# Attention with exponentials on two engines: two polynomial steps instead of three, and a looser limit on late fillers

## The chip, the core and the metric

The kernel runs on one core of a Trainium2 chip. A core has five engines that work side by side, each on its own queue of instructions and in order, and that wait for one another through semaphores: TensorE (PE in the profile, with its weight loads as PEld) for matmuls, VectorE (DVE) and ScalarE (ACT) for work on columns of up to 128 partitions, GpSimd (POOL), and SyncE (SP), which here issues DMA transfers. Matmul results land in PSUM, a small memory of eight banks of 512 fp32 columns per partition; all else lies in SBUF.

The metric is the device time in microseconds of one execution. The time before is 905.64 us, the median of 3 runs (905.61 to 906.5).

## The reference

One input x of 2048 tokens by 640 features goes through two halves, and a gate for each token mixes them. Inputs are bf16.

```python
def _A_ref(x, wqkv, wo):
    B, S, D = x.shape
    H = 32; Dh = D // H
    qkv = (lambda x, *d: x.transpose(*d))((x @ wqkv).reshape(B, S, 3, H, Dh), 2, 0, 3, 1, 4)
    q, k, v = qkv[0], qkv[1], qkv[2]
    scores = jnp.einsum("bhqd,bhkd->bhqk", q, k) * Dh ** -0.5
    p = _softmax(scores, axis=-1)
    o = jnp.einsum("bhqk,bhkd->bhqd", p, v)
    return (lambda x, *d: x.transpose(*d))(o, 0, 2, 1, 3).reshape(B, S, D) @ wo
def _B_ref(x, w1, b1, w2):
    h = jnp.einsum("bsd,df->bsf", x, w1) + b1
    sp = jnp.log1p(jnp.exp(-jnp.abs(h))) + jnp.where(h > 0, h, jnp.zeros_like(h))
    act = h * jnp.tanh(sp)
    return jnp.einsum("bsf,fd->bsd", act, w2)
x = A_x
g = _sigmoid((x * gate_w).sum(-1, keepdims=True))
return g * _A_ref(...) + (1 - g) * _B_ref(...)
```

Attention has 32 heads of 20 features each. Its softmax needs 32 x 2048 x 2048 exponentials, far more than anything else in the kernel asks of ScalarE or VectorE. The dense half has 1536 hidden features.

## The kernel before

**Units and steps.** Scores are computed transposed: keys on the 128 partitions, 512 queries in the columns. One such tile of one head is a *unit*: four blocks of queries (c), eight groups of four heads (g), sixteen tiles of keys (kt) and four heads in a group (j) make 2048 units. A *step* holds three units, which lie in three PSUM banks; two sets of three banks take turns. There are 683 steps, the last of two units. For each step, TensorE writes three scores (`emit_s`, line 1059), ScalarE takes the exponential of the step in one instruction (`emit_e`, line 1081), and TensorE multiplies the results by V into one PSUM bank, the four heads of a key tile side by side (`pv`, line 1184). V has a column of ones, so the sum for the softmax's denominator comes with it. When a group ends, VectorE copies the sums out and the group is divided by its denominators (`group_done`).

**Units on VectorE.** In some steps ScalarE takes only two of the three units, and VectorE computes the third exponential. Such a unit goes through these VectorE instructions, each over 512 columns (`emit_x`, from line 1092):
- the eviction (line 1098): score times a scale plus a bias, from PSUM to SBUF. The bias is chosen such that the bits of the fp32 result hold the exponential's exponent and a straight line in place of its mantissa;
- the mask (line 1113): the fraction, the low 14 bits of that word;
- three polynomial steps (line 1115): m = (m + constant) * m;
- the last step (line 1116): m times a small constant plus the evicted word, to an integer whose low 16 bits are the exponential in bf16.

The chains of two units run side by side in two lanes, on the scratch tiles EM and ER. The evicted words lie in five buffers, two of them in XE and three in a region that holds weights at another time: W2R at first, and REG later. The scores two steps later need the bank of the third unit, and so wait for the eviction as well as for ScalarE (`ev_op` in `emit_s`). The product of a finished unit with V is put in by `emit_off` in passes of its own.

**Who fixes the order.** The order of all instructions on all engines is worked out when the program is built. The class `Plan` keeps a clock for each engine, with a planned duration for each kind of instruction (0.60 for a wide VectorE instruction, 0.335 for a fast one, 1.335 for an exponential of three tiles and 0.908 for one of two), and records operations and what they depend on. The waits that are needed follow from that. So the durations in the source do not run on the chip, but they settle which instruction stands where in its queue.

**Fillers.** All other matmuls are tasks that are slipped in between scores and products: the projections for K, Q and V (`kq_task`, `k_task`, `v_pair_task` and their like), which are forced at the step in which they are due, squares for a bound on the scores (`sq_task`), the dense half's two products (`h_task`, `b_task`) and the output product (`p_task`, `part_task`). Their results are evicted by VectorE, and the activation of the dense half is a tanh on ScalarE (line 873) with a dozen VectorE instructions (`mish`). In each step the planner adds up the work of the tasks that can run, divides it by the steps left until each is due, and keeps the largest quotient as `behind`, in microseconds of TensorE work for a step.

**When a unit goes to VectorE.** While the first head group is worked on, `choose` alone decides: a buffer must be free, the work that lies queued for VectorE must be under 7 us, and the unit's chain must end before its group does; otherwise a unit of the next group may be taken. After that three more conditions stand before it: `behind` under `CATCH_UP`, no task more than 8 steps late, and enough VectorE time left for all that is still owed (`room`):

```python
compose(step + 2, choose(step + 2) if fast and step >= CALM and (step < slot_of(0, 1, 0)
        or behind < CATCH_UP and lag < LAG and room()) else None)
```

**Keeping TensorE's clock up.** `fill_up` repeats scores, or multiplies into a free bank, where the planned TensorE work of the last 3.41 us would fall under a share of 0.47.

A second program for scores too large for this method stands behind a flag; it isn't run with these inputs.

Of the kernel before, what the change touches and what calls it, by code (L numbers as in the profile page):

```python
# [64 lines left out]
AHEAD = 14  # L65
BEHIND = 7.0
PATIENCE = 10.0
CATCH_UP = 3.0
BUSY = 0.6
CROWD = 1.4  # L70
MARGIN = 0.5
# [24 lines left out]
ULPS = 128 / math.log(2)  # L96
BIAS = 65536 + 128 * 127
FRACTION = 0x3FFF
STEPS = (125802.5582306, -2329534004.47, 1.968676069154e20)
LAST_STEP = 4.153394027873e-38  # L100


class Op:
# [107 lines left out]
def bass_gated_mix__softmax_full_mha__dense_activation_mish__prompt_kernel(  # L211
# [91 lines left out]
    def ei(home):  # L303

        area, b = home
        return XE[:, b - 3, :] if b >= 3 else AREAS[area][1][:, b * CW:(b + 1) * CW]
# [13 lines left out]
    def scores(s):  # L320
        return PS[:, SLOT * (s % 2):SLOT * (s % 2 + 1), :]
# [7 lines left out]
    def attention(pl, fast):  # L329
# [48 lines left out]
        def slot_of(c, g, kt):  # L378
            return (first_unit[(c, g)] + kt * HG) // SLOT
# [6 lines left out]
        def dve(fn, deps=(), cost=0.1, kind="F"):  # L386

            ready = max([pl.now["dve"], *(d.t1 + HOP for d in deps if d is not None)])
            work(ready + (LATER if fast and now["rate"] < BUSY and now["bank"] else SLACK))
            return pl.add("dve", fn, deps, cost=cost, kind=kind)  # L390
# [638 lines left out]
        def compose(s, extra=None):  # L1029

            if extra:
                order.remove(extra)
                slots[s] = [order.popleft(), order.popleft(), extra]
            else:
                slots[s] = [order.popleft() for _ in range(min(SLOT, len(order)))]

        def emit_s(s):
            deps = [e_op.get(s - 2), ev_op.get(s - 2)]
            deps += [bank_free.get(SLOT * (s % 2) + i) for i in range(SLOT)] if s < 2 else []
            for c, g, kt, j in slots[s]:  # L1040
                if fast:
                    deps += [k_done[(real(g), subs(c, g, kt)[-1][0] // 4)], q_done[(real(g), c)]]
                if fast and (c, g) == (0, 0) and 2 <= kt < 4:
                    deps += k_more
            s_op[s] = score_mms(s, slots[s], deps)
            if any(u[0] < 2 for u in slots[s]):
                low_last[0] = s_op[s]
# [44 lines left out]
        def emit_x(s):  # L1092

            c, g, _, _ = slots[s][2]
            b = off[s]
            x = ei(b)
            y = x.bitcast(FP32)
            ev_op[s] = dve(lambda e: e.tensor_scalar(y, scores(s)[:, 2, :], SCALE * ULPS, BIAS, ALU.mult, ALU.add), [  # L1098
                s_op[s], ei_free[b], *(wkv_read if b[0] else ())], WIDE)
            last = [ev_op[s]]  # L1100
            ei_free[b] = "busy"
            lane = (nx[0] - 1) % LANES
            m = (EM, ER)[lane][:, :]
            f = m.bitcast(I32)
            ends = max((i for i, v in enumerate(islice(order, 80)) if v[:2] == (c, g)), default=0)
            due = pl.now["act"] + ends / TAKEN * EXP

            def piece(cost, fn, deps=lambda: ()):
                def run():
                    last[0] = pl.add("dve", fn, [last[0], *deps()], cost=cost)  # L1110
                soon[lane].append((cost, run, lambda: last[0], due))

            piece(FAST, lambda e: e.tensor_scalar(f, x, FRACTION, None, ALU.bitwise_and), lambda: [lane_last[lane]])
            for i in range(3):
                piece(WIDE, lambda e, v=m if i else f, i=i: e.scalar_tensor_tensor(m, v, STEPS[i], v, ALU.add, ALU.mult))  # L1115
            piece(WIDE, lambda e: e.scalar_tensor_tensor(x, m, LAST_STEP, y, ALU.mult, ALU.add))

            def end():
                lane_last[lane] = unit_done[slots[s][2]] = last[0]
            soon[lane].append((0.0, end, None, due))  # L1120

        def choose(s):

            late = max(0.0, pl.now["dve"] - pl.now["act"])
            urgent, other = (sum(t[0] for todo in some for t in todo) for some in ((norm, *soon), (blend, bg)))
            if (len(order) < SLOT or ei_free[home()] == "busy"
                    or late + urgent + other >= BEHIND):
                return None
            u = order[2]
            ends = max(i for i, v in enumerate(islice(order, 80)) if v[:2] == u[:2])  # L1130
            left = ends / TAKEN * EXP
            before = sum(t[0] for t in blend if t[3] < pl.now["act"] + left)
            if (late + urgent + before + CHAIN) * CROWD + MARGIN >= left:
                n = place[u[:2]] + 1
                js = [v[3] for v in islice(order, 2)]
                later_on = [v for v in islice(order, 3, 80) if n < len(groups) and v[:2] == groups[n] and v[2] < 2 and v[3] not in js]
                if not later_on:
                    return None
                u = later_on[0]
                need = [k_done.get((real(u[1]), 0)), q_done.get((real(u[1]), u[0]))]  # L1140
                if any(op is None or safe(op) > pl.now["pe"] for op in need):
                    return None
            off[s] = off_home[u] = home()
            nx[0] += 1
            off_units.setdefault(u[:2], []).append(u)
            return u
# [264 lines left out]
        def room():  # L1411

            step = now["step"]
            if step < start:
                return True
            owing = sum(t.dve for t in tasks) + sum(t[0] for todo in (norm, *soon, blend, bg) for t in todo)
            owing += 2 * MISH * len(acts) + GROUP * (len(order) // (NKT * HG) + 1) + CHAIN
            return owing + max(0.0, pl.now["dve"] - pl.now["act"]) < LOAD * (NSLOT - LAST - step) * EXP
# [35 lines left out]
        for step in range(NSLOT + 40):  # L1454
# [29 lines left out]
            if step + 2 < NSLOT:  # L1484
                compose(step + 2, choose(step + 2) if fast and step >= CALM and (step < slot_of(0, 1, 0) or behind < CATCH_UP and lag < LAG and room()) else None)
                emit_s(step + 2)
                to_come = pv_ready() * PASS
                if owed + rate > 0.1 and pick(pl.now["pe"] + 0.8):
                    to_come += min(owed + rate, 0.4)
                fill_up(to_come, False)  # L1490

                if fast and step + 2 in off:
                    emit_x(step + 2)
# [182 lines left out]
```

## Time and profile before

| | before |
|---|---|
| median of 3 runs | 905.64 us (905.61 to 906.5) |
| the profiled execution's own time | 901.96 us |
| its span, first to last instruction | 900.1 us |
| granted TensorE clock, mean | 0.995 |
| units on VectorE, of 2048 | 143 |

All views below come from one profiled execution, whose span is 1.86 us shorter than its own time. The page gives the busy time of each engine, its share of the span and the number of its instructions. A row of a group gives the line of the source, engine, operation, output and inputs by name, shapes and count; behind the first bar the busy time in us and the mean ns of one, behind the second the idle time of the engine before it and what ended that. Two instructions of one engine can overlap, so a mean duration may be longer than the distance between two starts; a row of one line of the source gives the first and the last start as well. A row of waits reads: engine, what it wrote, line, what it waited for, then us in total, times, and the longest. Rows of the order of time begin with the start in us from the start of the span and a length.

### The profile page before, as it was taken

What the parts mean: (1) busy time and instruction counts of PE and PEld (TensorE: products, weight loads), DVE (VectorE), ACT (ScalarE), POOL (GpSimd) and SP (SyncE); (2) the same over time, 40 slices, a digit from 0 to 9 for tenths busy, and PEclk for the clock granted to TensorE, in tenths of its full rate; (3) what the DMA queues carried; (4) which work ended last, traced back from release to release, by engine and by line L of the source; (5) the groups of instructions that cost most, each with busy time, mean ns of one, the idle gap of its engine ahead of it and who ended that gap; (6) DMA issues with size and microseconds to landing.
All of it is one profiled execution on the core that took longest, in us unless ns stands there. A gap on an engine that the chain in (4) does not pass through costs nothing.

```text
span 900.1 us, 15301 instructions
## 1 busy us (share of the span) xinstructions
PE 742.2 (82%) x6222; PEld 258.1 (29%) x6265; DVE 840.9 (93%) x1519; ACT 883.2 (98%) x714; POOL 15.3 (2%) x29
## 2 busy tenths in 40 slices
PE   8888778888888888788877878888888878888885
PEld 3222222222322233222222223232332323232232
DVE  5999999989799999999999999999999999979696
ACT  6999999999999999999999999999999999999996
POOL 2000000000000000000000000000000000000000
PEclk9999999999999999999999999999999999999999
DMA  9011200012022111031211120111221201200001
GB/s 215 22 48 55 67 24 13 3 34 68 25 66 77 57 45 42 13 110 32 56 36 43 53 72 19 54 39 32 58 60 42 65 20 54 60 20 24 15 13 35
DMA packets 69871, 42.45 MB, mean 47 GB/s; under 512 B 20472, under 2 KB 65776, under 8 KB 69744
## 3 DMA queue, kind: packets, MB, share of 16 engines
q1 hardware_dynamic: 67424, 40.89, 16.3%
q8 instruction: 52, 0.85, 0.4%
q10 hardware_dynamic: 2256, 0.47, 0.3%
q0 software_dynamic: 112, 0.01, 0.1%
q14 instruction: 27, 0.22, 0.1%
HBM read 33.97 MB, written 5.23 MB: 44 GB/s over the span
## 4 chain that ended last, share of the span: by engine, by line
ACT 95%; PE 2%; DMA 1%; DVE 1%; issue 0%; SPq 0%; ACTq 0%
ACT ETS L1081 92%; ACT REG L873 2%; DMA KT<-KS 1%; ACT W2R L873 1%; PE PS L1059 1%; DMA OTN<-in_A_x_dram 1%; PE PS L1184 0%; PE PS L910 0%; DVE HB L940 0%; PE PS L534 0%; PE PS L645 0%; DVE T L893 0%; DMA SUMS<-RR 0%; PE PS L654 0%; PE PS L934 0%
## 5 line engine op out<-in xcount | busy, mean ns | idle before, releaser
L1081 ACT ACTIVATE ETS<-PS 128x1536 bf16<-128x1536 f32 (+1 forms) x683 | 865.8, 1619 | 2.1 <-PE PS L1059 2.1
L1059 PE MATMUL PS<-QT,KT 32*128 32x512 bf16 (+1 forms) x2231 | 279.0, 378 | 142.3 <-ACT ETS L1081 127.9
L1184 PE MATMUL PS<-ETS,V_all 128*21 128x512 bf16 (+1 forms) x1963 | 211.6, 380 | 0.4 <-ACT ETS L1081 0.4
L1059 PEld LDWEIGHTS PS<-QT,KT 32*128 32x128 bf16 x2231 | 68.8, 91 | 355.4 <-ACT ETS L1081 334.5
L1115 DVE SCALAR_TENSOR_TENSOR EM<-EM 128x512 f32<-128x512 f32 (+1 forms) x216 | 146.9, 680 | 0.4
L1115 DVE SCALAR_TENSOR_TENSOR ER<-ER 128x512 f32<-128x512 f32 (+1 forms) x213 | 145.2, 682 | 0.2
L1184 PEld LDWEIGHTS PS<-ETS,V_all 128*21 128x21 bf16 x1963 | 49.7, 89 | 101.1 <-issue 96.0
L910 PE MATMUL PS<-W2R,HB 128*128 128x320 bf16 x384 | 73.2, 305 | 0.2 <-DVE XS L917 0.2
L841 PE MATMUL PS<-XB,REG 128*128 128x256 bf16 x360 | 53.6, 275 | 0.7 <-DVE HB L851 0.5
L534 PE MATMUL PS<-XB,WOQ 128*128 128x512 bf16 x135 | 41.9, 387 | 2.5 <-issue 1.6
L1098 DVE TENSOR_SCALAR XE<-PS 128x512 f32<-128x512 f32 x56 | 38.3, 684 | 5.2 <-PE PS L1059 5.0
L893 DVE RECIPROCAL T<-T 128x256 f32<-128x256 f32 x24 | 41.8, 1743 | 0.0
L910 PEld LDWEIGHTS PS<-W2R,HB 128*128 128x128 bf16 x384 | 29.7, 98 | 38.1 <-issue 24.3
L841 PEld LDWEIGHTS PS<-XB,REG 128*128 128x128 bf16 x360 | 29.4, 97 | 24.1 <-issue 21.8
L1098 DVE TENSOR_SCALAR REG<-PS 128x512 f32<-128x512 f32 x51 | 34.7, 681 | 1.7 <-PE PS L1059 1.4
L851 DVE TENSOR_TENSOR HB<-PS,B1F 128x512 bf16<-128x512 f32 x48 | 32.8, 683 | 2.4 <-PE PS L841 2.3
L1098 DVE TENSOR_SCALAR W2R<-PS 128x512 f32<-128x512 f32 x36 | 24.6, 684 | 5.1 <-PE PS L1059 4.7
L934 PE MATMUL PS<-WOQ,QT 128*128 128x320 bf16 x128 | 24.2, 302 | 1.1 <-DVE QT L1255 0.9
L934 PE MATMUL PS<-WOQ,OTN 128*128 128x320 bf16 x128 | 24.7, 302 | 0.3 <-DVE HB L851 0.3
L546 DVE CAST QT<-PS 128x512 bf16<-128x512 f32 x31 | 21.3, 686 | 3.1 <-PE PS L534 2.6
L707 PE MATMUL PS<-REG,XB 128*128 128x160 bf16 (+1 forms) x240 | 23.8, 234 | 0.3 <-DVE QT L546 0.2
L873 ACT ACTIVATE REG<-HB 128x1024 f32<-128x1024 bf16 x18 | 23.8, 1321 | 0.0
(124 smaller groups left out, 706.5 us busy)
## 6 DMA issues: line engine op xcount, KB each, us to landing
REG<-in_B_w_dram SPq DMA_DIRECT2D x36, 320.0 KB, 3.2
BCT<-SUMS SPq DMA_DIRECT2D x31, 256.0 KB
W2R<-in_B_w_dram SPq DMA_DIRECT2D x12, 320.0 KB, 3.3
KT<-KS SPq DMA_DIRECT2D x28, 128.0 KB
KS<-OTN SPq DMA_DIRECT2D x16, 128.0 KB, 1.7
W2R<-in_B_w_dram SPq DMA_DIRECT2D x1, 1920.0 KB, 8.3
out_dram<-OUTT SPq DMA_DIRECT2D x24, 80.0 KB, 1.6
REG<-in_A_wqkv_dram SPq DMA_DIRECT2D x2, 700.0 KB, 8.1
```

The costliest lines, as they stand in the source:

```text
L534: return lambda e, bank: e.matmul(PS[:, bank, :], pads[:, b, f, :], xt(c)[:, f, :], start=(f == 0), stop=(f == NFT - 1))
L841: return lambda e, bank: e.matmul(PS[:, bank, i * HW:(i + 1) * HW], w1b(n1)[:, f, i * P:(i + 1) * P], xt(c)[:, f, cols], start=(f == 0), s ...
L851: ev = dve(lambda e: e.tensor_tensor(hb, PS[:, bank, :].rearrange("p (i t) -> p i t", i=2), bias, ALU.add), [last, *b1f, *sq_read.values() ...
L873: ex = pl.add("act", lambda e: e.activation(U, h, AF.Tanh, scale=0.5), [ev, u_free[0]], cost=0.95)
L893: piece(RECIP, lambda e: e.reciprocal(T1[:, :], T1[:, :]))
L910: return lambda e, bank: e.matmul(PS[:, bank, 0:HALF], HB[:, hc % 2, f, t * P:(t + 1) * P], W2[:, f, half * HALF:(half + 1) * HALF], start ...
L934: return lambda e, bank: e.matmul(PS[:, bank, 0:HALF], otn(c, g, fast)[:, t * P:(t + 1) * P], WOG[:, g, half * HALF:(half + 1) * HALF], st ...
L1059: op = pl.add("pe", lambda e, i=i, g=real(g), tile=tile, j=j, cols=cols, c=c, of_q=of_q: e.matmul(scores(s)[:, i, cols], KT[32 * j:32 * j ...
L1081: e_op[s] = pl.add("act", lambda e: e.activation(ETS[:, s % NETS, 0:n, :], scores(s)[:, 0:n, :], AF.Exp, scale=SCALE), [s_op[s], pv_slot.g ...
L1098: ev_op[s] = dve(lambda e: e.tensor_scalar(y, scores(s)[:, 2, :], SCALE * ULPS, BIAS, ALU.mult, ALU.add), [s_op[s], ei_free[b], *(wkv_read ...
L1115: piece(WIDE, lambda e, v=m if i else f, i=i: e.scalar_tensor_tensor(m, v, STEPS[i], v, ALU.add, ALU.mult))
L1184: lasts[n] = pl.add("pe", lambda e, tile=tile, h=real(g) * HG + j, j=j, src=src[:, cols], of_q=of_q, count=count: e.matmul(PS[32 * j:32 * ...
```

## The change

VectorE's exponential loses one of its three polynomial steps; the constants of the two that stay and of the last step are others. The limit on `behind` up to which the planner still gives units to VectorE goes from 3 to 5. The plan that is built from this holds 169 units on VectorE, where it held 143. Planned durations, and the estimate of 3.6 us for a unit's chain in `choose` and `room` (`CHAIN`), are as they were.

```diff
-CATCH_UP = 3.0
+CATCH_UP = 5.0
...
-STEPS = (125802.5582306, -2329534004.47, 1.968676069154e20)
-LAST_STEP = 4.153394027873e-38
+STEPS = (128704.944057677, -2377933447.215862)
+LAST_STEP = 7.799623844033764e-18
...
             piece(FAST, lambda e: e.tensor_scalar(f, x, FRACTION, None, ALU.bitwise_and), lambda: [lane_last[lane]])
-            for i in range(3):
+            for i in range(len(STEPS)):
                 piece(WIDE, lambda e, v=m if i else f, i=i: e.scalar_tensor_tensor(m, v, STEPS[i], v, ALU.add, ALU.mult))
             piece(WIDE, lambda e: e.scalar_tensor_tensor(x, m, LAST_STEP, y, ALU.mult, ALU.add))
```

## The prediction, made before the result was known

> **What bounds the kernel now.** I read the head of the page first, then the chain of the work that ended last.
>
> ```profile
> span 900.1 us, 15301 instructions
> ...
> PE 742.2 (82%) x6222; PEld 258.1 (29%) x6265; DVE 840.9 (93%) x1519; ACT 883.2 (98%) x714; POOL 15.3 (2%) x29
> ...
> ACT 95%; PE 2%; DMA 1%; DVE 1%; issue 0%; SPq 0%; ACTq 0%
> ```
>
> ScalarE (ACT) is busy 98% of the span, and 95% of the chain lies on it. VectorE (DVE) is close behind at 93%, and PE has room. Who waited for whom says the same.
>
> ```profile
> PEld PS L1059 <- ACT ETS L1081: 334.5, 599, 1.5
> ...
> PE PS L1059 <- ACT ETS L1081: 127.9, 280, 1.2
> ...
> ACT ETS L1081 <- PE PS L1059: 2.1, 6, 0.5
> ...
> PE PS L1059 <- DVE XE L1098: 1.0, 2, 0.6
> ```
>
> TensorE stands before the score matmuls for ACT some 600 times. ACT stood idle for scores only six times, 2.1 us in all. So the span is a start, a train of exponentials, and an end. The train by its two forms (and one row of TensorE that is needed further down), in the grouping that keeps shapes apart, then the polynomial steps from the page's costliest groups:
>
> ```profile
> L1081 ACT ACTIVATE ETS<-PS 128x1536 bf16<-128x1536 f32 x539 | 775.5, 1708 | 1.5 <-PE PS L1059 1.5
> ...
> L1081 ACT ACTIVATE ETS<-PS 128x1024 bf16<-128x1024 f32 x144 | 181.5, 1289 | 0.6 <-PE PS L1059 0.6
> ...
> L1184 PE MATMUL PS<-XE,V_all 128*21 128x512 bf16 x54 | 18.3, 400 | 0.0
> ```
>
> ```profile
> L1115 DVE SCALAR_TENSOR_TENSOR EM<-EM 128x512 f32<-128x512 f32 (+1 forms) x216 | 146.9, 680 | 0.4
> L1115 DVE SCALAR_TENSOR_TENSOR ER<-ER 128x512 f32<-128x512 f32 (+1 forms) x213 | 145.2, 682 | 0.2
> ```
>
> 216 + 213 = 429 polynomial steps, three for each of 143 units on DVE. A unit that DVE takes turns a three-tile exponential (1536 columns, a triple) into a two-tile one (1024, a pair). 143 pairs, plus the last step, which has two tiles left (2048 = 682 x 3 + 2), give the 144 of the row.
>
> The mean durations (1708, 1289 ns) overlap from one instruction to the next, so they are no price. I take starts instead, from the rows of line 1081: first the whole run, then a stretch of triples alone, then a mixed stretch without a visible stall.
>
> ```profile
> L1081 ACT ACTIVATE ETS<-PS x683: 1015/1709/2079, 10.4 to 890.3; 128x1536 bf16<-128x1536 f32 x136, 128x1024 bf16<-128x1024 f32 x35
> ```
>
> ```profile
> L1081 ACT ACTIVATE ETS<-PS x19: 1452/1567/1687, 823.2 to 847.1; 128x1536 bf16<-128x1536 f32 x19
> ```
>
> ```profile
> L1081 ACT ACTIVATE ETS<-PS x48: 1092/1692/1816, 37.8 to 95.9; 128x1536 bf16<-128x1536 f32 x37, 128x1024 bf16<-128x1024 f32 x11
> ```
>
> ```profile
> L873 ACT ACTIVATE REG<-HB x18: 1047/1354/1588, 448.0 to 821.3; 128x1024 f32<-128x1024 bf16 x18
> L873 ACT ACTIVATE W2R<-HB x6: 1051/1330/1423, 209.3 to 364.8; 128x1024 f32<-128x1024 bf16 x6
> ```
>
> ```profile
> 448.46 0.94 ACT REG L873
> ```
>
> A triple: 23.9 us over 18 intervals, 1.33 us. A pair without stalls: 58.1 us hold 36 triples and 11 pairs (the last start, a triple, opens no interval), so (58.1 - 47.9)/11 = 0.93 us. A pair on average: 879.9 us from first to last start, less 24 tanh at 0.94 = 22.6, leaves 857.3; less 539 x 1.33 = 716.9 leaves 140.4 for 143 pairs, 0.98 us. Every stall of the train is in that 0.98, wherever it fell.
>
> **The change part by part.**
>
> *The step taken out.* 143 x 1 polynomial step leave DVE. DVE's order of time, in a dense place, gives the price:
>
> ```profile
> 769.92 0.68 DVE L1098 TENSOR_SCALAR REG<-PS 128x512 f32<-128x512 f32 x1
> 770.52 0.68 DVE L903 SCALAR_TENSOR_TENSOR HB<-REG,HB 128x512 bf16<-128x512 f32 x1
> ...
> 771.72 0.42 DVE L1113 TENSOR_SCALAR ER<-XE 128x512 int32<-128x512 int32 x1
> 772.05 0.68 DVE L1115 SCALAR_TENSOR_TENSOR EM<-EM 128x512 f32<-128x512 f32 x1
> 772.66 0.68 DVE L1115 SCALAR_TENSOR_TENSOR ER<-ER 128x512 f32<-128x512 int32 x1
> ```
>
> Starts are 0.60 us apart after a wide instruction and 0.33 after the mask of line 1113. A unit (eviction, mask, three steps, last step) costs 5 x 0.60 + 0.33 = 3.33 us, and 2.73 after. DVE is rid of 143 x 0.60 = 86 us. By itself this moves the end by nothing: ACT's train hides it, and ACT waits for DVE only through TensorE (1.0 us, row above). That the two new constants stand for three changes no shape and no time.
>
> *The 26 units more.* They cost DVE 26 x 2.73 = 71 us, less than the 86 set free, so its load falls by 15 us. Is there room where it is needed? By stage, after the time columns come PE, PEld, DVE, ACT:
>
> ```profile
> 10.00:200.00 190.00, 155.06 (x1333) 49.78 (x1352) 171.98 (x326) 189.10 (x153) 6.52 (x12) 0.99 0.18 48
> 200.00:340.00 140.00, 116.69 (x967) 41.20 (x979) 130.54 (x234) 139.36 (x113) 3.21 (x6) 1.00 0.19 55
> 340.00:700.00 360.00, 297.95 (x2424) 102.89 (x2432) 356.13 (x638) 359.79 (x292) 0.52 (x1) 1.00 0.17 48
> 700.00:892.00 192.00, 162.73 (x1452) 59.50 (x1455) 173.98 (x309) 191.35 (x153) 0.00 (x0) 1.00 0.11 33
> ```
>
> From 340 to 700 DVE is full (356 of 360): there only the freed time pays for units. Elsewhere it idles 18 + 9 + 18 = 45 us beside what is freed. In all, 86/2.73 = 31 units would fit into the freed time alone, and 26 are asked.
>
> ACT loses a third of a triple 26 times. Bounds: 1.33 - 0.93 = 0.40 us each if the new pairs do not stall, 10.4 us; 1.33 - 0.98 = 0.35 if they draw stalls as today's do, 9.1 us. No row shows what a denser mix draws, so a gain of nothing stays possible and is a rival. I take 0.37, between the two, because part of the stalls in the 0.98 belongs to no pair: **26 x 0.37 = 9.6 us**.
>
> The row above is all that the trace needs here; a page gives the same term another way. The Trainium skill, "ScalarE: Activation LUTs", section "What ACT_TABLE_LOAD costs", has an ACTIVATE stream one column per cycle at 1.2 GHz, whatever the function; an estimate from that is 512/1.2 = 427 ns a tile and 11.1 us for 26, so 894.5 us. The trace's 0.40 is a little below that and its 0.35 well below, since the page prices the stream and not the stalls behind it.
>
> *PE.* It keeps every score and every product with V. A unit finished on DVE can no longer ride in the pass of its four heads, so at most 26 more passes. Bounds: nothing where several units share one, and 0.40 us each by the row of line 1184 with XE above, 10 us on an engine that idles 158 (900.1 - 742.2). They are hidden under ACT as long as the 128 us of TensorE's waits for it last; without that cover it would be the whole 10 us. I take nothing.
>
> *The allowance (3.0 to 5.0 us of filler work per step).* It adds no instruction; it lets units be chosen where they were refused, and the fillers (projections, dense half, output) come later. What is late then has its due step as a limit: forced ones go out in a block. I price it at nothing, with its loss as a rival. SP's and POOL's queues get nothing new and lose nothing.
>
> *TensorE's clock.* A short stretch ran at a granted clock of 0.50 (the third number from the end of the row), and ACT's order of time across it shows a stall:
>
> ```profile
> 696.60:700.00 3.40, 3.40 (x18) 0.84 (x13) 3.25 (x5) 3.19 (x3) 0.00 (x0) 0.50 0.13 33
> ```
>
> ```profile
> 691.54 7.14 ACT L1081 ACTIVATE ETS<-PS 128x1536 bf16<-128x1536 f32 x5
> 698.88 1.45 ACT L1081 ACTIVATE ETS<-PS 128x1536 bf16<-128x1536 f32 x1 [0.21 <-PE PS L1059]
> 700.59 9.71 ACT L1081 ACTIVATE ETS<-PS 128x1536 bf16<-128x1536 f32 x8 [0.26 <-PE PS L1059]
> ```
>
> From 691.54 to 700.59 there are six triples, 9.05 us where 6 x 1.33 = 8.0 would do: 1.1 us for one such stretch. Another order of the work may be without it or have two more: 2 us to the worse, 1 to the better, for the range, and nothing in the sum.
>
> *The ends.* 10.4 us before the train and 900.1 - 890.3 = 9.8 after its last start stay.
>
> **Sum.** Span 900.1 - 9.6 = 890.5 us. The profiled execution took 901.96, 1.86 more than its span, and the median of the runs is 905.64, 3.68 above that. I carry both offsets: 892.4 for a profiled execution, and **896.0 us** for the median. A measurement of this kernel can tell about 0.2%, 1.8 us, from no change: below 903.8 is faster.
>
> **The rivals.**
>
> *Fewer stalls as well.* DVE with 15 us less to do evicts and delivers sooner, and the 0.05 us that an average pair loses goes for all 169: 905.6 - 10.4 - 143 x 0.05 = 888 at best, 891 if half. For it: the full stage 340 to 700. Against: ACT waits are put down to scores, hardly to DVE.
>
> *Evictions late.* The scores two steps later need the third tile evicted by DVE (line 1098). If each of 169 evictions holds TensorE 0.03 us longer, 5 us are lost: 901. For it: 93% of DVE's time stays taken. Against: today that wait is 1.0 us over 143.
>
> *It does not do what it says.* The 26 tiles leave ACT, but at places where scores are not ready, so ACT stands instead: 905.6, no change. Against: ACT is full in all four stages.
>
> *Slower: blocks of late fillers.* While projections for K, Q and V run (to about 340 us), a task at its due step goes out whole, ahead of the next scores. More lag, more blocks, and a pair gives TensorE 0.93 us for what had 1.33. ACT's waits for scores cost 2.1/6 = 0.35 us each now. 27 more of them eat 9.6 us; from there on the kernel is slower, and 35 more give 908. For it: even 3.0 us of work per step is more than a step holds, so the old limit allowed blocks too. Against: six waits today, and TensorE stands idle 35 of the first 190 us.
>
> **How the numbers follow.** Forecast (893 to 899, with the page's figure in it): 0.60. Fewer stalls (below 893): 0.10. Evictions late (899 to 903.8): 0.13. No effect: 0.06. Slower: 0.11. Faster is 0.60 + 0.10 + 0.13 = 0.83, same 0.06, slower 0.11. A range from 890.5 to 904 leaves out the two last (0.17) and about 0.03 of the best case; its own width covers 0.35 to 0.40 a pair and the clock stretches.
>
> **What would show it.** Right: 170 pairs and 513 triples on line 1081, 338 steps on line 1115 at 0.68 us, ACT's train from about 10.4 to 880.7, triples still 1.33 apart, ACT at 98%, DVE at 93% or below. The eviction case would show as TensorE waiting for line 1098 by more than 5 us, the block case as over 20 waits of ACT for scores before 340 us. A train that shortens by 9.6 us with an end longer than 9.8 would mean that fillers were left over behind the last exponential, which I have at nothing.

## The result and the profile after

The changed kernel takes 890.01 us, the median of 6 runs (889.84 to 890.31); the kernel before took 905.62 us in the same session, the median of 6 (903.88 to 907.57). The ratio is 0.9829, with a 95% interval from 0.9811 to 0.9847: 15.6 us faster, where 9.6 were forecast, and 0.5 us below the low end of the range.

The head of the page of after, the chain that ended last, and the polynomial steps:

```profile
span 888.0 us, 15315 instructions
...
PE 751.6 (85%) x6246; PEld 258.7 (29%) x6246; DVE 828.4 (93%) x1506; ACT 872.1 (98%) x714; POOL 16.0 (2%) x29
...
ACT 97%; PE 2%; DVE 0%; issue 0%; ACTq 0%
...
L1115 DVE SCALAR_TENSOR_TENSOR EM<-EM 128x512 f32<-128x512 int32 (+1 forms) x170 | 115.7, 680 | 0.2
L1115 DVE SCALAR_TENSOR_TENSOR ER<-ER 128x512 f32<-128x512 int32 (+1 forms) x168 | 114.5, 682 | 0.1
```

ScalarE is the bound as before. There are 170 + 168 = 338 steps, two for each of 169 units, as the forecast said, and VectorE's busy time fell by 12.5 us (840.9 to 828.4; forecast 15). The train of exponentials by form, in the grouping that keeps shapes apart, and then its first and last start:

```profile
L1081 ACT ACTIVATE ETS<-PS 128x1536 bf16<-128x1536 f32 x513 | 729.1, 1674 | 1.2 <-PE PS L1059 1.2
...
L1081 ACT ACTIVATE ETS<-PS 128x1024 bf16<-128x1024 f32 x170 | 197.7, 1236 | 0.0
```

```profile
L1081 ACT ACTIVATE ETS<-PS x683: 1018/1592/2116, 10.0 to 878.2; 128x1536 bf16<-128x1536 f32 x126, 128x1024 bf16<-128x1024 f32 x45
```

513 triples and 170 pairs, exactly as forecast, but the train lasts 878.2 - 10.0 = 868.2 us where 870.3 was forecast (879.9 - 9.6). It begins 0.4 us earlier, and the end behind its last start is 888.0 - 878.2 = 9.8 us as it was. So the span lost 12.1 us: 11.7 from the train and 0.4 from the start. The waits and the stages of after (in the stages: start and end, length, then PE, PEld, DVE, ACT, POOL, clock, DMA):

```profile
PE PS L1059 <- ACT ETS L1081: 110.0, 256, 1.1
...
ACT ETS L1081 <- PE PS L1059: 1.2, 2, 0.7
```

```profile
10.00:200.00 190.00, 160.92 (x1367) 51.21 (x1365) 171.39 (x327) 189.99 (x156) 6.76 (x13) 1.00 0.18 49
200.00:340.00 140.00, 120.52 (x1004) 42.33 (x1004) 132.89 (x243) 140.00 (x116) 3.35 (x5) 1.00 0.18 53
340.00:700.00 360.00, 305.38 (x2461) 104.80 (x2457) 353.06 (x635) 359.25 (x297) 0.52 (x1) 0.99 0.18 50
700.00:882.00 182.00, 156.16 (x1374) 56.70 (x1374) 164.46 (x292) 179.48 (x146) 0.00 (x0) 1.00 0.10 30
```

ACT waits for scores twice, not six times, so no block of fillers stands in its way. VectorE stays full from 340 to 700 us. TensorE shows as busier in every stage (0.85, 0.86, 0.85 and 0.86 of the time, where it was 0.82, 0.83, 0.83 and 0.85), but a part of that is only the record: 43 of the 6265 matmuls of before are missing from its trace (6222 there, 6265 in the trace of the run before again).

The medians are 15.6 us apart and the two profiled spans 12.1. The other 3.5 us are the second miss: the profiled execution of before was 3.7 us faster than its median, and that of after only 0.2 faster. So of the 6.0 us between the 896.0 that was forecast and the 890.0 that was measured, 2.1 are the train, 0.4 its start and 3.5 the offset. Two questions are left for the experiments: why a unit was worth more than 0.37 us, and what the offset was.

### The profile page after: what moved, and what is told of

Same layout as the page of the kernel before. It is cut to its first block, busy times and chain, and to the rows that moved or that the text cites. A ratio compares the mean times of both kernels' runs of the same rounds, so it can differ in the third digit from the quotient of the medians.

```text
span 888.0 us, 15315 instructions
## 1 busy us (share of the span) xinstructions
PE 751.6 (85%) x6246; PEld 258.7 (29%) x6246; DVE 828.4 (93%) x1506; ACT 872.1 (98%) x714; POOL 16.0 (2%) x29
## 3 DMA queue, kind: packets, MB, share of 16 engines
q1 hardware_dynamic: 67424, 40.89, 16.4%
## 4 chain that ended last, share of the span: by engine, by line
ACT 97%; PE 2%; DVE 0%; issue 0%; ACTq 0%
ACT ETS L1081 95%; ACT REG L873 2%; ACT W2R L873 1%; PE PS L486 1%; PE PS L1436 0%; PE PS L1059 0%; PE PS L910 0%; PE PS L654 0%; PE PS L1184 0%; PE PS L645 0%; DVE HB L940 0%; PE PS L934 0%; PE PS L633 0%; ACT KT L629 0%; DVE ETS L473 0%
## 5 line engine op out<-in xcount | busy, mean ns | idle before, releaser
L1081 ACT ACTIVATE ETS<-PS 128x1536 bf16<-128x1536 f32 (+1 forms) x683 | 854.8, 1565 | 1.2 <-PE PS L1059 1.2
L1184 PE MATMUL PS<-ETS,V_all 128*21 128x512 bf16 (+1 forms) x1935 | 208.7, 381 | 0.6 <-ACT ETS L1081 0.5
L1115 DVE SCALAR_TENSOR_TENSOR EM<-EM 128x512 f32<-128x512 int32 (+1 forms) x170 | 115.7, 680 | 0.2
L1115 DVE SCALAR_TENSOR_TENSOR ER<-ER 128x512 f32<-128x512 int32 (+1 forms) x168 | 114.5, 682 | 0.1
L1098 DVE TENSOR_SCALAR XE<-PS 128x512 f32<-128x512 f32 x67 | 45.8, 684 | 5.4 <-PE PS L1059 4.4
L534 PE MATMUL PS<-XB,WOQ 128*128 128x512 bf16 x155 | 46.6, 384 | 0.2 <-DVE OTN L594 0.2
L1098 DVE TENSOR_SCALAR REG<-PS 128x512 f32<-128x512 f32 x58 | 39.4, 681 | 1.6 <-PE PS L1059 1.2
L1098 DVE TENSOR_SCALAR W2R<-PS 128x512 f32<-128x512 f32 x44 | 30.0, 683 | 3.6 <-PE PS L1059 3.3
L586 PE MATMUL PS<-XB,REG 128*128 128x512 bf16 x80 | 24.4, 384 | 0.0
L889 DVE SCALAR_TENSOR_TENSOR REG<-REG 128x1024 f32<-128x1024 f32 x18 | 21.9, 1214 | 2.6 <-ACT REG L873 2.6
```

The source lines that it names most:

```text
L534: return lambda e, bank: e.matmul(PS[:, bank, :], pads[:, b, f, :], xt(c)[:, f, :], start=(f == 0), stop=(f == NFT - 1))
L1081: e_op[s] = pl.add("act", lambda e: e.activation(ETS[:, s % NETS, 0:n, :], scores(s)[:, 0:n, :], AF.Exp, scale=SCALE), [s_op[s], pv_slot.g ...
L1184: lasts[n] = pl.add("pe", lambda e, tile=tile, h=real(g) * HG + j, j=j, src=src[:, cols], of_q=of_q, count=count: e.matmul(PS[32 * j:32 * ...
```

## The experiments

All times are medians of the kernel and of the kernel before in the same session. The changed kernel itself was run in the first session alone, so a difference from its 890.01 us holds to about the 1.5 us by which before varies between sessions. The clock is the mean of TensorE's granted clock over all runs of a row; the first row has the 0.986 of 35 runs of before that were made together later, and the six runs of after gave 0.993 to 0.998. The train is that of the profiled execution, whose own clock can lie elsewhere (0.995 in the first profile of before, 0.977 in before again).

The last two columns are worked out from the starts in each trace. From the start of a triple to the next start on ACT, the median distance is 1.33 us in every trace; from a pair's start it is 0.90 us in nine of the thirteen traces (96 of the 169 pairs of after lie within 3 ns of 0.904). What the distances of a train have beyond 1.330 and 0.904 is called its stalls here. "At half clock" is the part of the stalls whose exponentials start between 1.4 us before and 1.5 us after a stretch of granted clock 0.50.

| run | units | us | before, same session | clock | train, us | stalls, us | of these at half clock |
|---|---|---|---|---|---|---|---|
| before (first profile) | 143 | 905.62 | | 0.986 | 879.9 | 10.9 | 2.0 |
| after | 169 | 890.01 | 905.62 | 0.996 | 868.2 | 10.3 | 1.3 |
| before again | 143 | 905.27 | 904.10 | 0.985 | 885.3 | 16.4 | 10.4 |
| step out, same order | 143 | 905.66 | 904.10 | 0.985 | 880.4 | 11.4 | 2.7 |
| fewer units | 109 | 918.39 | 904.10 | 0.988 | 895.3 | 11.9 | 4.6 |
| unplanned third step | 169 | 904.20 | 904.10 | 0.988 | 879.5 | 21.6 | 2.2 |
| two steps, limit 3 | 162 | 893.25 | 904.32 | 0.996 | 871.5 | 10.7 | 1.4 |
| three steps, limit 5 | 140 | 908.70 | 904.32 | 0.984 | 887.1 | 16.9 | 8.1 |
| before, no filling | 143 | 913.95 | 904.32 | 0.947 | 891.5 | 22.5 | 16.9 |
| after, no filling | 169 | 899.30 | 904.32 | 0.961 | 876.3 | 18.4 | 11.0 |
| before, more filling | 140 | 904.52 | 905.16 | 0.992 | 883.2 | 12.9 | 3.2 |
| one step | 197 | 880.92 | 905.16 | 0.995 | 858.3 | 12.4 | 0.6 |
| one step, replanned | 207 | 875.59 | 905.16 | 0.994 | 853.1 | 11.4 | 1.5 |

**Before again.** No edit.

> The kernel before, unchanged, for another profile and more executions. The profile of before took 901.96 us, 3.7 us less than its median; that of after took 889.84, only 0.2 less than its median. Theory A: the earlier profile caught a lucky execution; executions of this kernel differ by how many short stretches TensorE runs at half clock (about 1.1 us each) and by waits that differ from run to run. Then this profile lies anywhere between 902 and 907 us, its span about 1.9 us below its own time, and a longer span goes with more half-clock stretches or with longer waits of ACT for scores. Theory B: a fixed offset of 3.7 us between a profiled execution and the others of this kernel. Then span 900.1 and time 902 again, with the median at 905.6.

The profiled execution took 907.98 us, 1 us beyond the 902 to 907 of theory A, with a span of 906.1 and a mean clock of 0.977. Theory B's fixed offset is out, and the cause that theory A names holds. Nine half-clock stretches lie in this train. The view by stretches shows three of them, each as a pair, a sparse stretch and the one behind it (the columns are those of the stages above; the third number from the end is the clock):

```profile
146.60:150.10 3.50, 2.26 (x24) 0.55 (x21) 3.46 (x7) 3.50 (x4) 0.00 (x0) 1.00 0.02 2
150.20:153.60 3.40, 3.40 (x18) 0.67 (x16) 2.34 (x5) 3.08 (x3) 0.00 (x0) 0.51 0.03 2
266.00:269.60 3.60, 1.97 (x16) 0.70 (x15) 3.60 (x7) 3.60 (x4) 0.00 (x0) 1.00 0.37 122
269.70:273.10 3.40, 3.40 (x20) 0.78 (x21) 1.80 (x3) 2.06 (x3) 0.00 (x0) 0.50 0.11 32
716.80:720.20 3.40, 2.15 (x21) 0.65 (x20) 3.40 (x6) 3.40 (x3) 0.00 (x0) 1.00 0.36 107
720.30:723.70 3.40, 3.40 (x20) 1.16 (x17) 1.87 (x5) 3.07 (x3) 0.00 (x0) 0.50 0.01 3
```

In the 3.4 to 3.6 us ahead of these stretches, TensorE was busy for 0.55 to 0.65 of the time (2.26/3.50, 1.97/3.60, 2.15/3.40), against 0.85 over the train (750.22 us from 10 to 895). In the half-clock stretch behind, it is busy all the time, ACT stands for part of it (2.06 us busy of 3.40 in the middle pair), and the train is late: by 0.0 to 2.3 us around each of the nine, 10.4 us in all. The first profile of before has two of them, with 2.0 us. In this execution ACT waited for scores 6.6 us in ten places:

```profile
ACT ETS L1081 <- PE PS L1059: 6.6, 10, 1.3
```

Over the 35 runs of the kernel before that were made together, the 12 with a clock of 0.990 or more average 903.4 us at 0.991, and the 9 at 0.980 or less average 906.8 at 0.979: 0.28 us for each thousandth of clock, and a straight line through all 35 gives 0.27. The first profile of before was at 0.995, one of the best that occur; the four later runs of this kernel that were granted 0.995 took 901.49 to 902.71 us, as it did (901.96). The usual clock, 0.986, costs about 9 x 0.27 = 2.4 us more. The time outside the span is 1.8 to 2.0 us in every run (907.98 - 906.1 = 1.9 here).

**The step taken out, order and units kept.** The plan is made with three steps; then the third is taken out of it:

```diff
-            for i in range(3):
+            for i in range(2):
                 piece(WIDE, lambda ...)
+            piece(WIDE, None)
...
+    for op in fast.ops:
+        op.deps = [r for d in op.deps for r in (d.deps if d.fn is None else [d])]
+    fast.ops = [op for op in fast.ops if op.fn is not None]
```

> The plan of before with its 143 units and its order on every engine, from which the third polynomial step is taken out after planning (constants of the change). DVE loses 143 x 0.60 = 86 us and nothing else changes. Theory A (the forecast's step): nothing on the path, 905.6 us within 1.8, ACT's train 879.9 us within 2. Theory B: stalls of the train come from late VectorE work; then the train falls by several of the 10.4 us by which it exceeds 539 x 1.33 + 143 x 0.904 + 24 x 0.94, and the time by 3 us or more.

905.66 us, a ratio to before of 1.0017 (1.0003 to 1.0031). VectorE's busy time falls from 840.9 to 770.0 us and its share to 85%, and nothing is gained: the train is 880.4 us, with the same few waits of ACT.

```profile
PE 752.7 (84%) x6265; PEld 258.0 (29%) x6265; DVE 770.0 (85%) x1376; ACT 883.3 (98%) x714; POOL 15.0 (2%) x29
```

The shorter polynomial pays only through the units that the planner puts in its place, as forecast. The run also shows that VectorE's lighter load is not what raised the clock (0.985).

**Fewer units.** The changed kernel with at least six steps between two units on VectorE:

```diff
-            if (len(order) < SLOT or ei_free[home()] == "busy"
+            if (len(order) < SLOT or s < spaced[0] or ei_free[home()] == "busy"
...
+            spaced[0] = s + 6
             off[s] = off_home[u] = home()
```

> The changed kernel with a distance of at least 6 steps between two units on VectorE: 109 units in place of 169. Price of a unit. The forecast's price of 0.37 us (stalls go with the pairs): 60 x 0.37 = 22 us longer than 890.0, so 912.2. The price without stalls, 1.330 - 0.904 = 0.426: 25.6 us, so 915.6, and the train's excess over its clean sum stays near the 10.4 us that it has with 143 and with 169 units. If stalls go with pairs, the excess falls to about 6.5 us.

918.39 us, above both. The line of the exponential (1082 here):

```profile
L1082 ACT ACTIVATE ETS<-PS x683: 1016/1762/1865, 10.1 to 905.4; 128x1536 bf16<-128x1536 f32 x139, 128x1024 bf16<-128x1024 f32 x32
```

The train is 895.3 us, 27.1 longer than with 169 units: 0.45 us a unit, of which the longer stalls (11.9 for 10.3 us) are 0.03. Of the 2.8 us above the second figure, some 2 are clock (0.988 against 0.996, at 0.27 a thousandth). By the forecast's reckoning, an average pair here costs (895.3 - 22.6 - 573 x 1.33)/109 = 1.01 us; with 143 units it was 0.98 and with 169 it is (868.2 - 22.6 - 513 x 1.33)/169 = 0.97. The average pair gets cheaper as pairs are added, so most of the stalls in it belong to the train and not to the pairs. The table says the same: with 109, 143, 162 and 169 units the stalls outside half clock are 7.3, 8.9, 9.3 and 9.0 us.

**An unplanned third step.** The plan of after, in which one unit in four gets the three old steps, the third put in after planning:

```diff
+    ops = []
+    for op in fast.ops:
+        if op in thirds:
+            op.deps = [Op("dve", lambda e, m=thirds[op]: e.scalar_tensor_tensor(m, m, STEPS3[2], m, ALU.add, ALU.mult), op.deps, None)]
+            ops.append(op.deps[0])
+        ops.append(op)
```

> The plan of after, 169 units in the same order, but one unit in four is computed with the three old steps, the third of which is put in after planning: some 42 unplanned instructions of 0.60 us, 25 us more on VectorE, whose idle time in the 888 us is 60 us. If VectorE's lateness costs nothing (the forecast took nothing): 890.0 within 1.8. If late evictions and deliveries reach the train (the rival 'evictions late'): TensorE waits for lines 1098 and 1116, ACT for scores, and the time grows by 5 us or more; at the very most by the 25.

904.20 us: 42 instructions that the plan did not know of (1548 on VectorE against 1506) cost 14.2 us, more than half of their 42 x 0.60 = 25 us, though VectorE is then busy only 95% of the span. Some 3 of the 14.2 us go with the lower clock of most of these runs: at a like clock, the two profiled executions are 11.2 us apart (901.06 at 0.994, 889.84 at 0.993), and the stalls outside half clock grow from 9.0 to 19.4 us. The waits tell how (line numbers are up to 8 higher here: 1084 is the exponential, 1062 the scores, 1101 the eviction, 1123 the last step, 913 and 844 fillers):

```profile
ACT ETS L1084 <- PE PS L1062: 7.5, 20, 0.8
...
PEld PS L913 <- DVE XB L920: 7.0, 12, 1.3
...
PE PS L844 <- DVE HB L854: 4.7, 10, 1.0
...
PEld PS L1192 <- DVE XE L1123: 3.1, 6, 0.9
...
PE PS L1062 <- DVE REG L1101: 2.3, 4, 0.9
```

TensorE waits for evictions of fillers' results, for finished units and for evicted scores, and what is late there reaches ACT 20 times in place of 2. The mechanism of the rival "evictions late" is real, and VectorE's idle time does not cover it. It did not occur in the change: there TensorE's waits for evictions and finished units of VectorE's chain (lines 1098 and 1116) come to 2.5 us in all, none of them before a score. That this is so because the plan knew of each instruction is the reading that fits; no run tests it apart.

**Each part alone.** `CATCH_UP = 3.0` with the two steps, and `CATCH_UP = 5.0` with the three.

> The changed polynomial alone, with the limit on late fillers back at 3.0: 162 units in place of 169. Theory A (units times 0.426 us, nothing else): 890.0 + 7 x 0.426 = 893.0 us. Theory B (the looser limit costs waits that the added units pay for, or brings more than units): a time that differs from 893.0 by more than 2 us, with the train's excess over its clean sum other than 10 to 11 us.

893.25 us with 162 units, as theory A has it.

> The looser limit alone, three polynomial steps kept: 140 units in place of 143. Theory A: 3 x 0.426 = 1.3 us longer than before, 905.4 to 906.9, because VectorE's time and not the limit is what holds the units down. Theory B (the limit itself pays): below 903.

908.70 us, a ratio of 1.0048 (1.0036 to 1.0061), with 140 units. Theory B is out: the limit alone makes the kernel slower. It is 4.4 us and not 1.3 above the kernel before. By 0.27 us a thousandth, about 1 of the rest is clock (0.984 against 0.987 in its session). The profile points to more of it: 8.1 us of stalls at half clock, while the stalls outside are 8.8 us, as in the first profile of before (8.9). So late fillers show no price of their own here, but some 2 us between the medians stay unexplained. So the polynomial brings 19 of the 26 units, and the limit 7 more once the polynomial is short.

**Without filling.** `STREAM = 0.0` in each of the two kernels.

> The kernel before without the repeated scores and the matmuls into a free bank that keep TensorE's clock up; 143 units as before. Theory A (the 3.5 us by which before's median exceeds its first profile are half-clock stretches of TensorE): mean granted clock falls below 0.98, the train's excess rises from 10.9 us by about 0.2 to 0.3 us for each thousandth of clock, the time goes to 910 or more. Theory B (the clock does not reach the train): time within 2 us of before at whatever clock.

> The kernel after without that filling; 169 units. Theory A (after runs at a higher clock because the same matmuls stand closer together): its clock falls less than that of the kernel before without filling, and its time rises by less; forecast 892 to 896 us. Theory B (after's clock is up by chance of where the filling stands): it falls as far as in the other, and the difference of the two kernels without filling is 26 x 0.426 = 11 us and no more.

Before: 913.95 us at 0.947; after: 899.30 us at 0.961.

```profile
10.00:890.00 880.00, 739.94 (x5910) 248.56 (x5909) 821.56 (x1481) 869.59 (x699) 10.45 (x19) 0.95 0.16 45
```

```profile
10.00:880.00 870.00, 734.56 (x5961) 248.36 (x5955) 813.12 (x1481) 863.22 (x703) 10.99 (x19) 0.96 0.16 46
```

For before, theory A holds: 40 thousandths less clock than in its session cost 9.6 us, 0.24 each, and the stalls grow to 22.5 us, 16.9 of them at half clock. For after, both figures miss: its clock falls by 35 thousandths, nearly as far, and it takes 899 us where A had 892 to 896. But its lead is there without any filling: 0.961 against 0.947. The two kernels are then 14.7 us apart, more than theory B's 11; the 14 thousandths between their clocks, at 0.24 to 0.27, are 3.4 to 3.8 us and cover that. So the filling does not make the lead in clock.

**More filling for before.** `STREAM = 0.53`.

> The kernel before with filling up to a planned share of 0.53 in place of 0.47; the plan then holds 140 units on VectorE, 3 fewer, which cost 1.3 us by 0.426 each. Theory A (half-clock stretches follow stretches of about 3.4 us in which TensorE is busy for 0.55 to 0.67 of the time, and before has more such stretches than after): the clock rises from 0.986 to 0.99 or more, at 0.27 us a thousandth; the runs lie closer together, and in spite of the 3 units the median is 903 to 905. Theory B (the clock follows the density of matmuls over the whole span, or chance): clock as before, 906 or more.

904.52 us at a clock of 0.992, with runs from 902.4 to 906.9. The clock can be raised by filling, as theory A has it (though the sparse stretches ahead of the three half-clock ones left here were busy for 0.44, 0.70 and 0.80 of 3.4 us, so its 0.55 to 0.67 is no limit), but 3 fewer units take 1.3 us back, and the ratio to before is 0.9996 (0.9979 to 1.0013): nothing that can be told from no change.

**One polynomial step.** The two constants become `STEPS = (-16384.0,)` and `LAST_STEP = 1.6417503356933594e-07`, a parabola in the fraction; worked out over all 16384 values of the fraction, its greatest error against 2 to the power of the fraction is 0.49 of a unit in the last place of bf16, where the two steps have 0.015.

> The changed kernel with one polynomial step in place of two, (f - 16384) * f times a constant: 197 units by the same planner settings. Theory A (0.426 us a unit as long as the plan holds): 890.0 - 28 x 0.426 = 878.1 us, the train's excess at 10 to 11 us, clock 0.995. Theory B (the denser mix draws stalls at last; TensorE has 0.90 us in a pair for what had 1.33): excess above 14 us and the time above 881.

880.92 us: between the two theories. The train shrinks by 9.9 us for 28 units, 0.35 each; one wait of 1.2 us, at 240 us, stands out. The stalls are 12.4 us, 2.1 more than in after.

> One polynomial step, and planner settings chosen anew (a chain taken at 2.7 us, VectorE's queue at 6 us, fillers up to 10 steps late, due steps of the dense half moved): 207 units. Theory A: 890.0 - 38 x 0.426 = 873.8 us. Theory B: as in the run before, above 878.

875.59 us, a ratio to before of 0.9685 (0.9658 to 0.9712) and 14.4 us below the changed kernel. This beats both kernels, and lies between the two theories, nearer to A. Beside the settings that the expectation names, five more were chosen anew (`BUSY`, `CROWD`, `EAGER`, `END`, `SHIFT`), so the run tests no single one of them. The train, 853.1 us, is 15.1 below after's for 38 units, 0.40 each.

```profile
L1081 ACT ACTIVATE ETS<-PS x683: 1018/1512/2013, 10.2 to 863.4; 128x1536 bf16<-128x1536 f32 x124, 128x1024 bf16<-128x1024 f32 x47
```

## Why the prediction was right, and where it was wrong

**What bounds the kernel, and that the removed step is worth nothing by itself:** right, and shown by taking the step out with all else kept.

**The count of units and forms, VectorE's account:** right. 169 units fit with VectorE still at 93%.

**The price of a unit, 0.37 us in the sum:** too small; this step failed by its size. "Every stall of the train is in that 0.98" made the lower bound, 0.35, and half of the doubt was kept in the value taken. The upper bound, 0.40, was too low as well: its 0.93 for a pair came from a stretch "without a visible stall" in which, by the single starts, five of the eleven pairs take 0.90 us and the other six 0.93 to 0.95. Without any stall the price is 1.330 - 0.904 = 0.426 us. The runs agree: from 109 to 207 units the train goes from 895.3 to 853.1 us, 42.2/98 = 0.43. Between neighbours it varies (0.46 by the medians from 162 to 169 units, 0.35 by the trains from 169 to 197), so 0.43 is an average. At 0.43 the 26 units are worth 11.2 us; the trains differ by 11.7. The stalls stayed with the train: 10.9 us of them before and 10.3 after, of which 2.0 and 1.3 are at half clock. The figure that was worked out from a page lay nearest: by the estimate from the Trainium skill, "ScalarE: Activation LUTs", section "What ACT_TABLE_LOAD costs", 427 ns a tile and 11.1 us. The measured slope, 0.43, agrees with it. The prediction said that the page lay above the trace because it leaves stalls out, but it was the trace's reading that had stalls in it.

**"I carry both offsets":** wrong, and the larger miss. It took the 3.68 us between the profiled execution and the median for a constant. They go with the half-clock stretches, whose number differs from run to run: before's first profile ran at 0.995, its runs at 0.986. The changed kernel's runs are at 0.993 to 0.998, and its median is 0.2 us from its profile. At 0.27 us a thousandth the nine or ten thousandths between the kernels make about 2.5 of the 3.5 us. That is an estimate: the 0.27 was measured on before, and in the six runs of after the time does not follow the clock (889.84 us at 0.993, 890.00 at 0.998). What is left is within the spread of before, whose medians in four sessions lay from 904.1 to 905.6. At a clock of 0.995, before takes about 902.2 us (four runs) and after 890.0: there the change is worth about 12.2 us.

**The term for the clock, "nothing in the sum":** the price is about right, 1.1 us for the one stretch it read, where three traces of before have 0.6 to 1.0 on average for each 3.4 us at half clock (16.9 us for 28 such lengths without filling, 10.4 for 11 in before again, 2.0 for two in the first). In the two profiles the number hardly changed either, two such lengths before and three after. What was wrong is that one execution's number was taken for the kernel's: before usually has more, and so its median hid a loss that the changed kernel does not have.

**Rivals.** "Fewer stalls" was the case that came nearest in time (888 to 891), but its mechanism is not what happened: with VectorE much lighter, the train stayed at 880 us, and the stalls of after are 0.6 us shorter, not several. "Evictions late" is a real price, some 11 us at a like clock, that this change did not have to pay. "No effect" and "blocks of late fillers" fell: two waits of ACT for scores in all, and the limit at 5 with two steps brings 893.25 - 890.01 = 3.2 us for 7 units, 0.46 each.

**Open:** why after, and the other plans with a shorter polynomial and many units, run at a higher clock. It is neither the filling (the lead stays without it) nor VectorE's lighter load (taking the step out left 0.985), nor the number of units alone (109 units with two steps ran at 0.988, above before's 0.986). Sparse stretches of TensorE go ahead of the half-clock ones that were looked at, but what in the plans makes these rarer over many runs was not separated.

## What to carry to other kernels

Where one engine runs a gapless train, price a change by the slope between starts of its forms, and leave the stalls out unless a row ties them to the instruction that is added. Before carrying over the distance between a profiled execution and the median, ask whether it is a constant: look at the granted clock of the single runs. In an order that is fixed at build time, time freed on a second engine is worth nothing until the plan spends it, and a few unplanned instructions can cost about half of their length (11 of 25 us at a like clock here) even where that engine seems to have room.

## What the runs showed of the hardware

In the run before again, TensorE's clock halved nine times within the train, for 3.4 us or twice that. In the 3.4 us ahead it was busy for 0.51 to 0.67 of the time, with no gap longer than 0.95 us. The share at which the clock falls is not shown: in the run with more filling, 0.44, 0.70 and 0.80 went ahead. The Trainium skill, "TensorE: Matmul & The Clock Gate", Part 1, names in its table of the two states an idle window of about 3.4 us as the condition; the length agrees, but the rows here show that a window without any long gap is enough.
